# The stores of the last token group: which queue issues them, and in how many pieces

## The chip, the core and the metric

The kernel runs on one core of one Trainium2 chip. The metric is device time in microseconds for one execution of the whole program. TensorE (PE) multiplies matrices, VectorE (DVE) and ScalarE (ACT) work on elements, GpSimd (POOL) and SyncE (SP) mainly issue DMAs. A DMA is issued by an instruction on an engine's own queue (here SyncE's or ScalarE's for stores) and is then carried out by 16 DMA engines that all queues share.

## The reference

Sigmoid attention, and behind it a gated feed-forward layer, for 8 batches, 12 heads, 448 positions and 64 numbers per head:

```python
scores = scale * np.matmul(q, k.transpose(0, 1, 3, 2)) - np.log(S)
attn = 1.0 / (1.0 + np.exp(-scores))
attn_out = np.matmul(attn, v)
x = attn_out.transpose(0, 2, 1, 3).reshape(B * S, H * D)      # 3584 x 768
out = (np.maximum(x @ w_gate, 0.0) * (x @ w_val)) @ w_out     # 768 -> 1536 -> 768
```

The result is 3584 x 768 in float32, 11.0 MB.

## The kernel before, in words

Batches are taken in groups of two. For each batch the attention is computed in 16 bits (`qk_unit`, `pv_group`), and its output, transposed, feeds the gate and value products (`gv`, `gv_pair`) of the group. The gated product `hT` of a group of two batches is then multiplied by `w_out` in `down_pair`. That function takes two blocks of 128 tokens at a time (`y1` and `y2`, each a buffer of 128 x 768 float32 from a pool of four, `ysb`) and computes their column halves `lo` (0 to 384) and `hi` (384 to 768) from seven products instead of eight, with sums of the operands prepared on VectorE. ScalarE copies the first product of each half out of the accumulation bank into `y1` or `y2` (`scaled_act`, line 451), VectorE adds the others (`plus`, line 469). A later product may add onto the bank that such a copy reads, so TensorE then waits for the copy.

The order of all instructions is the order in which the Python code issues them (`manual_schedule`); each engine runs its own list from front to back. The group loop runs through `next_work`, and what remains at the end is the last group (`LAST`, batches 6 and 7): four calls of `down_pair` in a row with nothing else beside them. The first of these pairs the last block of the group before with one block of the last group; the other three take the remaining six blocks.

`store` (lines 350 to 363) writes a block to `out`. Outside the last group it is called with `(nc.sync, nc.sync)` and issues two DMAs of 64 rows each on SyncE, because the rows of the two halves lie in different places. In the last group the 128 rows of a block form one pattern. There, line 353 first removes repeated engines, and then the rows are divided among the engines that are left: `(nc.sync, nc.sync)` becomes a single DMA of 128 rows on SyncE, `(nc.sync, nc.scalar)` one DMA of 64 rows on each.

The very last `down_pair` (`last` is true) stores piece by piece, as soon as each is complete:

1. `y1` left half (line 527): SyncE, 128 rows x 384.
2. `y2` right half (line 532): SyncE 64 rows, ScalarE 64 rows, x 384.
3. `y1` right half (line 536): SyncE 64 rows, ScalarE 64 rows, x 384.
4. `y2` left half in two quarters of 192 columns, each with its own product of 12 half-width matmuls in all, its own addition on VectorE (line 545) and its own store (line 549): both on SyncE.

The stores and transposes of SyncE and ScalarE count on eight semaphores, 0 to 7, each DMA taking the next one in turn; before a semaphore is used again its earlier DMA must have landed. In the built program of this kernel, `y1`'s left half counts on number 4, `y2`'s right half on 5 and 6, `y1`'s right half on 0 (SyncE) and 7 (ScalarE), the two quarters on 1 and 2. When SyncE has issued everything it waits for these eight semaphores one after the other in the order 0 to 7, each with an instruction of its own, then drains, and the engines meet in a barrier that ends the program (line 1062 in the profile, the launch).

Of the kernel before, what the change touches and what calls it, by code (L numbers as in the profile page):

```python
# [18 lines left out]
def kernel(  # L19
# [10 lines left out]
    nc = tc.nc  # L30

    B, H, S, D = q.shape
    DM, DF = moe_w_gate.shape
# [43 lines left out]
    def bank(name, shape=(P, 512), dtype=FP32):  # L77
        pool, tag = free[0]
        free.rotate(-1)
        return pool.tile(list(shape), dtype, tag=tag, name=name)  # L80
# [4 lines left out]
    def later(order):  # L85
        keys = [free[i - 8] for i in order]
        for key in keys:
            free.remove(key)
            free.append(key)
# [260 lines left out]
    def store(g, t, ysb, m0, m1, engines):  # L350
        if g == LAST:
            dst = out[2 * g * S : 2 * (g + 1) * S, m0:m1].rearrange("(b t c) m -> c t b m", b=2, c=NCH)[t]
            engines = list(dict.fromkeys(engines))
            n = P // len(engines)
            for i, eng in enumerate(engines):
                rows = slice(i * n, (i + 1) * n)
                eng.dma_start(dst[i * n // 2 : (i + 1) * n // 2], ysb[rows, m0:m1])
            return
        for i, eng in enumerate(engines):
            j = 2 * t + i  # L360
            b, c = 2 * g + j // NCH, j % NCH
            dst = out[b * S : (b + 1) * S, m0:m1].rearrange("(t c) m -> c t m", c=NCH)[c]
            eng.dma_start(dst, ysb[64 * i : 64 * i + 64, m0:m1])
# [3 lines left out]
    HF, HM, HD = NFC // 2, DM // 2, NDC // 2  # L367
# [19 lines left out]
    def products(jobs):  # L387
        for ps, n, kn, A, W, first in jobs:
            for k_ in range(kn):
                nc.tensor.matmul(  # L390
                    ps[:, 0:n],
                    A[:, k_, :],
                    W[:, k_, :],
                    start=(first and k_ == 0),
                    stop=(k_ == kn - 1),
                    skip_group_check=True,
                )
# [21 lines left out]
    def tiles_in(g, p):  # L419
        return ((g - 1, 2 * p), (g, 2 * p)) if p == NPP else ((g, 2 * p), (g, 2 * p + 1))  # L420

    def token_blocks(g, p):
        blocks = []
        for gt, t in tiles_in(g, p):
            h = odd[gt] if gt < g else hT_tiles[g][:, :, t * P : (t + 1) * P]
            blocks += [h[:, 0:HF, :], h[:, HF:NFC, :]]
        return blocks
# [22 lines left out]
    def scaled_act(o, ps):  # L450
        nc.scalar.activation(o, ps[:, 0:HM], AF.Copy, scale=OUT_SCALE)  # L451

    def down_pair(g, p, beside, then, last, first_copy, amid=None):
        A11, A12, S3, A22 = token_blocks(g, p)
        S1, S2, S4 = sums.pop(("y", g, p))
        T1, T2, T3, T4 = late["T"]
        B11, B21, B22 = wo[:, 0:HF, 0:HM], wo[:, HF:NFC, 0:HM], wo[:, HF:NFC, HM:DM]
        y1, y2 = (ysbp.tile([P, DM], FP32, tag="ysb", name="ysb") for _ in range(2))
        lo, hi = slice(0, HM), slice(HM, DM)
        b, c = bank("u"), bank("y12")  # L460
        if not amid or (g, p) in SUMS_LATE:
            a = bank("y11")
            later((7, 6, 5))

        def product(ps, A, W, first=True):
            products([(ps, HM, HF, A, W, first)])

        def plus(o, ps):
            nc.vector.scalar_tensor_tensor(  # L469
                out=o, in0=ps[:, 0:HM], scalar=OUT_SCALE, in1=o, op0=AOP.mult, op1=AOP.add  # L470
            )

        first, second = tiles_in(g, p)

        product(b, A11, B11)
        first_copy(y1[:, lo], b)
        beside()
        if (g, p) in SUMS_LATE:
            product(a, A12, B21)
            plus(y1[:, lo], a)  # L480
            product(c, S1, T1)
            scaled_act(y2[:, hi], c)
            product(b, S2, T2, False)
            scaled_act(y1[:, hi], b)
            product(c, S4, B22, False)
            plus(y1[:, hi], c)
            store(*first, y1, 0, DM, (nc.sync, nc.sync))
            steps = ()
            if amid:
                amid()  # L490
                steps = prepare_steps()
                for step in steps[:2]:
                    step()
            product(b, S3, T3, False)
            plus(y2[:, hi], b)
            (scaled if amid else scaled_act)(y2[:, lo], b)
            d = bank("y21")
            if amid:
                later((0, 6, 7))
            else:  # L500
                then()
            product(d, A22, T4)
            plus(y2[:, lo], d)
            for step in steps[2:]:
                step()
            store(*second, y2, 0, DM, (nc.sync, nc.sync))
            return
        product(c, S1, T1)
        scaled_act(y2[:, hi], c)
        product(b, S2, T2, False)  # L510
        scaled_act(y1[:, hi], b)
        if amid:
            product(c, S4, B22, False)
            plus(y1[:, hi], c)
            amid()
            product(b, S3, T3, False)
            plus(y2[:, hi], b)
            later((0,))
            a = bank("y11")
            later((6,))  # L520
            product(a, A12, B21)
            plus(y1[:, lo], a)
        else:
            product(a, A12, B21)
            plus(y1[:, lo], a)
            if last:
                store(*first, y1, 0, HM, (nc.sync, nc.sync))
            product(b, S3, T3, False)
            plus(y2[:, hi], b)
            if last:  # L530
                scaled_act(y2[:, lo], b)
                store(*second, y2, HM, DM, (nc.sync, nc.scalar))
            product(c, S4, B22, False)
            plus(y1[:, hi], c)
        if last:
            store(*first, y1, HM, DM, (nc.sync, nc.scalar))
        else:
            store(*first, y1, 0, DM, (nc.sync, nc.sync))
        then()
        if last:  # L540
            for m0 in (0, HM // 2):
                m1 = m0 + HM // 2
                d = bank("y21")
                products([(d, HM // 2, HF, A22, T4[:, :, m0:m1], True)])
                nc.vector.scalar_tensor_tensor(
                    out=y2[:, m0:m1], in0=d[:, 0 : HM // 2], scalar=OUT_SCALE, in1=y2[:, m0:m1],
                    op0=AOP.mult, op1=AOP.add,
                )
                store(*second, y2, m0, m1, (nc.sync,))
        else:  # L550
            product(b, A22, T4, False)
            scaled_act(y2[:, lo], b)
            store(*second, y2, 0, DM, (nc.sync, nc.sync))
# [342 lines left out]
    def prepare_steps():  # L896
        if work:
            kind, g, i = work[0]
            if kind == "w":
                return unit_sum_steps(("w", g, i), i, sums_tile(2 * P))  # L900
            if kind == "y" and (g, i) != (0, 0):
                return token_sum_steps(g, i, 0, HF - 2 if FRESH.get(g) == i else HF)
        return ()
# [5 lines left out]
    def next_work(jobs=(), alone=False, amid=None, ahead=()):  # L909
        kind, g, i = work.popleft()  # L910

        due = pending[:]
        del pending[:]

        def beside():
            for job in due + list(jobs):
                job()

        for job in ahead:
            job()  # L920
        if kind == "y":
            down_pair(g, i, beside, prepare, not work, scaled_act if alone else scaled, amid)
        elif amid:
            raise ValueError(kind)
        elif kind == "w":
            by = (nc.vector.tensor_copy, nc.scalar.copy)
            gv_pair(g, i, lambda: (prepare(), beside()), (by[alone], by[alone or bool(ahead)]))
        elif kind == "s":
            gv_split(g, i, lambda: (prepare(), beside()))
        else:  # L930
            gv(g, 0, S, i, True)
            beside()
            prepare()
# [133 lines left out]
```

## Time and profile before

| | before |
|---|---|
| time, median of 3 runs | 388.93 us (388.58 to 389.41) |
| the profiled execution's own time | 388.44 us |
| its span in the profile | 386.7 us |
| TensorE busy | 380.4 us, 98% of the span |
| VectorE busy | 305.0 us, 79% |
| ScalarE busy | 227.2 us, 59% |
| GpSimd busy | 49.8 us, 13% |
| granted TensorE clock | 1.0 |
| data moved | HBM read 47.19 MB, written 11.01 MB |

A time of a run is some 1.7 us longer than the span of the same execution; what lies around the span is start and end. In the timeline a row gives the start in us from the span's start, the duration, the engine, the source line, the operation, what it writes and reads, and in brackets how long the engine stood idle before it and what released it. `SPq` and `ACTq` are the queues of SyncE and ScalarE: the duration of a `DMA_DIRECT2D` there is the time that the issuing instruction took, not the transfer. The transfer's end is seen in the list of issues as the time from issue to landing, and its data in the busy share of the DMA engines.

### The profile page before, as it was taken

Reading aid. Unit: us, or ns where it says so; the run is one execution under the profiler, and the core shown is the slowest. Engines: PE = TensorE matmul, PEld = TensorE weight load, DVE = VectorE, ACT = ScalarE, POOL = GpSimd, SP = SyncE. Lnnn points to the kernel's source line nnn. Section 1 sums busy time; section 2 is a strip of 40 time slices with the busy share of each in tenths; the row PEclk is TensorE's granted clock in tenths of the full one; section 3 lists DMA queues with packets and bytes.
Section 4 is the critical chain, followed back from the end, with each engine's and each line's share of the span. In section 5 each row is a group of like instructions: output and inputs, shape, how many; then the busy total and the mean of one; then the engine's idle time right before and its main releaser. Section 6 shows DMA issues by size and latency. Waiting matters only on the chain.

```text
span 386.7 us, 8967 instructions
## 1 busy us (share of the span) xinstructions
PE 380.4 (98%) x3570; PEld 222.9 (58%) x3570; DVE 305.0 (79%) x611; ACT 227.2 (59%) x480; POOL 49.8 (13%) x73
## 2 busy tenths in 40 slices
PE   8999999999999999999999999999999999999995
PEld 6778776885555545555555554555555555555663
DVE  3455667769868999999868789999988788999662
ACT  5967887568777645555777764555577343333321
POOL 9633307100400003000300300000000000000000
PEclk9999999999999999999999999999999999999999
DMA  9999999999979303962599892222013220000224
GB/s 179 198 199 204 203 187 163 208 208 131 186 162 178 81 2 39 165 109 47 49 231 236 157 234 44 49 49 49 0 43 83 65 60 0 2 0 2 82 102 145
DMA packets 67483, 43.81 MB, mean 113 GB/s; under 512 B 35568, under 2 KB 64112, under 8 KB 67440
## 3 DMA queue, kind: packets, MB, share of 16 engines
q0 software_dynamic: 28960, 23.24, 39.4%
q1 hardware_dynamic: 37776, 19.34, 23.6%
q10 hardware_dynamic: 704, 0.66, 0.5%
q8 instruction: 28, 0.46, 0.5%
q14 instruction: 15, 0.12, 0.1%
HBM read 47.19 MB, written 11.01 MB: 151 GB/s over the span
## 4 chain that ended last, share of the span: by engine, by line
PE 96%; ACT 2%; DMA 1%; DVE 1%; issue 0%; ACTq 0%
PE u L390 35%; PE g L390 16%; PE y L390 12%; PE qk_ps L239 10%; PE pv_ps L257 8%; PE g_ps L322 5%; PE v_ps L322 5%; PE u L719 2%; PE g L719 2%; ACT PT L187 2%; PE trt L204 1%; DMA ysb<-in_k_dram 1%; DVE qkT L211 0%; DVE q L792 0%; PE warm_ps L175 0%
## 5 line engine op out<-in xcount | busy, mean ns | idle before, releaser
L187 ACT ACTIVATE PT<-qk_ps 128x448 f16<-128x448 f32 (+3 forms) x318 | 151.0, 586 | 78.7 <-PE qk_ps L239 78.5
L390 PEld LDWEIGHTS <-S 128*128 128x128 f16 x576 | 56.3, 98 | 45.9
L629 DVE TENSOR_TENSOR gsb<-g,gsb 128x448 f32<-128x448 f32 x72 | 42.8, 624 | 7.8 <-PE g L390 7.5
L239 PE MATMUL qk_ps<-qkT 64*64 64x448 f16 (+2 forms) x756 | 47.3, 336 | 0.6 <-ACT PT L187 0.3
L390 PEld LDWEIGHTS <-hT 128*128 128x128 f16 x318 | 29.5, 98 | 24.1 <-issue 6.1
L257 PE MATMUL pv_ps<-PT,v 64*64 64x448 f16 (+2 forms) x756 | 36.4, 329 | 0.2 <-ACT PT L187 0.2
L469 DVE SCALAR_TENSOR_TENSOR ysb<-y,ysb 128x384 f32<-128x384 f32 x33 | 18.3, 556 | 20.6 <-PE y L390 14.0
L184 DVE TENSOR_SCALAR xT<-pv_ps 128x448 f16<-128x448 f32 (+2 forms) x53 | 27.8, 567 | 7.5 <-PE pv_ps L257 6.3
L390 PEld LDWEIGHTS <-wg 128*128 128x128 f16 x216 | 20.1, 98 | 21.8 <-issue 4.3
L390 PEld LDWEIGHTS <-wv 128*128 128x128 f16 x216 | 21.1, 98 | 19.7
L451 ACT ACTIVATE ysb<-u 128x384 f32<-128x384 f32 x28 | 13.7, 490 | 30.9 <-PE u L390 26.8
L390 PE MATMUL u<-wo,hT 128*128 128x384 f16 x156 | 29.8, 328 | 0.0
L239 PEld LDWEIGHTS <-qkT 64*64 64x64 f16 x756 | 17.7, 105 | 20.6 <-issue 14.0
L111 POOL DMA_DIRECT2D k<-in_k_dram x14 | 10.9, 775 | 141.4 <-DVE rel L222 135.6
L257 PEld LDWEIGHTS <-v 64*64 64x64 f16 x756 | 21.4, 107 | 11.1 <-issue 0.6
L390 PE MATMUL u<-xT,wg 128*128 128x448 f16 x108 | 23.5, 354 | 0.0
L390 PE MATMUL g<-xT,wg 128*128 128x448 f16 x108 | 23.4, 353 | 0.0
L390 PE MATMUL g<-xT,S 128*128 128x448 f16 x108 | 23.4, 353 | 0.0
L390 PE MATMUL u<-X,S 128*128 128x448 f16 x108 | 23.4, 353 | 0.0
L390 PE MATMUL g<-X,S 128*128 128x448 f16 x108 | 23.4, 353 | 0.0
L390 PE MATMUL u<-xT,wv 128*128 128x448 f16 x108 | 23.4, 353 | 0.0
L390 PE MATMUL u<-X,wv 128*128 128x448 f16 x108 | 23.4, 353 | 0.0
(98 smaller groups left out, 563.7 us busy)
## 6 DMA issues: line engine op xcount, KB each, us to landing
out_dram<-ysb SPq DMA_DIRECT2D x43, 192.0 KB, 3.6
v<-in_v_dram POOLq DMA_DIRECT2D x8, 336.0 KB, 15.6
v<-in_v_dram POOLq DMA_DIRECT2D x16, 168.0 KB, 15.6
k<-in_k_dram POOLq DMA_DIRECT2D x4, 672.0 KB, 11.8
q<-in_q_dram POOLq DMA_DIRECT2D x4, 672.0 KB, 15.2
wo<-in_moe_w_out_dram POOLq DMA_DIRECT2D x2, 1152.0 KB, 19.1
k<-in_k_dram POOLq DMA_DIRECT2D x9, 224.0 KB, 11.6
out_dram<-ysb SPq DMA_DIRECT2D x5, 384.0 KB, 2.7
```

The source lines that it names most:

```text
L111: nc.gpsimd.dma_start(t16[:, xs, cs], rows_of(src, b)[:, xs, cs])
L184: nc.vector.tensor_scalar(out=xT, in0=src, scalar1=XSCALE, scalar2=None, op0=AOP.mult)
L187: nc.scalar.activation(PT_ap, ps_ap, AF.Sigmoid, bias=sig_bias, scale=qk_scale)
L204: nc.tensor.transpose(trt[64 * h : 64 * h + 64, c * P : (c + 1) * P], t16[:, 2 * g + h, c * D : (c + 1) * D], ident[:],)
L239: nc.tensor.matmul(out_of(hh)[o : o + 64, :], qkT[rows, c, cols], qkT[rows, NCH + c0 : NCH + c1, cols], start=True, stop=True, tile_positi ...
L257: nc.tensor.matmul(ps[hh][64 * r : 64 * r + 64, 0:qn], v16[rows, 2 * g + hh, c * D : (c + 1) * D], pieces[c][rows, hh, :], start=(c == 0), ...
L322: nc.tensor.matmul(ps[:, 0:qn], (wg, wv)[i][:, dc, f * P : (f + 1) * P], xT_tiles[b][:, dc, q0 : q0 + qn], start=(dc == 0), stop=(dc == ND ...
L390: nc.tensor.matmul(ps[:, 0:n], A[:, k_, :], W[:, k_, :], start=(first and k_ == 0), stop=(k_ == kn - 1), skip_group_check=True,)
L451: nc.scalar.activation(o, ps[:, 0:HM], AF.Copy, scale=OUT_SCALE)
L469: nc.vector.scalar_tensor_tensor(out=o, in0=ps[:, 0:HM], scalar=OUT_SCALE, in1=o, op0=AOP.mult, op1=AOP.add)
L629: nc.vector.tensor_tensor(out=gs[u][i][:], in0=ps[u][:, 0:S], in1=gs[u][i][:], op=AOP.add)
L719: nc.tensor.matmul(ps[j // 2][:, j % 2 * SQ : (j % 2 + 1) * SQ], sets[j][i][:, k_, :], W[:, k_, :], start=(first and j % 2 == 0 and k_ == ...
```

## The change

Three places change. `store` no longer removes repeated engines, so `(nc.sync, nc.sync)` gives two DMAs of 64 rows each on SyncE in the last group too: that holds for its five whole blocks and for `y1`'s left half. `y1`'s right half goes as one DMA of 128 rows on SyncE. Of the two quarters of `y2`'s left half the first is stored by ScalarE, the second by SyncE as before. `y2`'s right half stays with one DMA on each.

```diff
@@ def store(g, t, ysb, m0, m1, engines):
         if g == LAST:
             dst = out[2 * g * S : 2 * (g + 1) * S, m0:m1].rearrange("(b t c) m -> c t b m", b=2, c=NCH)[t]
-            engines = list(dict.fromkeys(engines))
             n = P // len(engines)
             for i, eng in enumerate(engines):
                 rows = slice(i * n, (i + 1) * n)
@@ def down_pair(...):
         if last:
-            store(*first, y1, HM, DM, (nc.sync, nc.scalar))
+            store(*first, y1, HM, DM, (nc.sync,))
         else:
             store(*first, y1, 0, DM, (nc.sync, nc.sync))
         then()
@@
-                store(*second, y2, m0, m1, (nc.sync,))
+                store(*second, y2, m0, m1, (nc.sync if m0 else nc.scalar,))
```

In the built program SyncE then issues 15 stores in the last group instead of 10, ScalarE two as before. The instructions of TensorE, VectorE and GpSimd are the same in number and order. The semaphores move on accordingly: `y1`'s left half counts on 1 and 2, `y2`'s right half on 3 and 4, `y1`'s right half on 5, ScalarE's quarter on 6 and the last store on 7.

## The prediction

> **What bounds the kernel now.** I read the page first, then the chain of waits over the last 27 us, then every store of the last 7 us one by one.
>
> ```profile
> span 386.7 us, 8967 instructions
> PE 380.4 (98%) x3570; PEld 222.9 (58%) x3570; DVE 305.0 (79%) x611; ACT 227.2 (59%) x480; POOL 49.8 (13%) x73
> PE 96%; ACT 2%; DMA 1%; DVE 1%; issue 0%; ACTq 0%
> ...
> 380.46 1.98 PE y L390 x18
> 382.44 0.02 issue
> 382.46 0.36 DVE ysb L545
> ```
>
> TensorE is busy for 98% of the span and carries 96% of the chain. The change gives TensorE, VectorE and GpSimd no new instruction, so all but the end of these 386.7 us stays if no buffer comes free too late (last rival). The chain reaches TensorE's last product at 382.44 and VectorE's last piece at 382.82 (382.46 + 0.36). From there to 386.7 there are only stores and the end of the program: 3.9 us, the only stretch where the change can pay. Its rows, from the timeline (start, duration) and the list of DMA issues (KB, us to landing):
>
> ```profile
> 381.54 0.56 DVE L469 SCALAR_TENSOR_TENSOR ysb<-y,ysb 128x384 f32<-128x384 f32 x1 [0.43 <-PE y L390]
> 382.03 0.36 DVE L545 SCALAR_TENSOR_TENSOR ysb<-y,ysb 128x192 f32<-128x192 f32 x1
> 382.46 0.36 DVE L545 SCALAR_TENSOR_TENSOR ysb<-y,ysb 128x192 f32<-128x192 f32 x1
> ...
> 380.16 0.54 SPq L357 DMA_DIRECT2D out_dram<-ysb  x1
> 381.14 0.55 SPq L357 DMA_DIRECT2D out_dram<-ysb  x1
> 382.12 0.55 SPq L357 DMA_DIRECT2D out_dram<-ysb  x1
> 382.76 0.55 SPq L357 DMA_DIRECT2D out_dram<-ysb  x1
> 383.41 0.57 SPq L357 DMA_DIRECT2D out_dram<-ysb  x1
> 381.15 0.63 ACTq L357 DMA_DIRECT2D out_dram<-ysb  x1
> 382.13 0.57 ACTq L357 DMA_DIRECT2D out_dram<-ysb  x1
> ...
> out_dram<-ysb SPq DMA_DIRECT2D x1, 192.0 KB, 2.2
> out_dram<-ysb SPq DMA_DIRECT2D x1, 96.0 KB, 2.2
> out_dram<-ysb SPq DMA_DIRECT2D x1, 96.0 KB, 2.0
> out_dram<-ysb ACTq DMA_DIRECT2D x1, 96.0 KB, 2.4
> out_dram<-ysb ACTq DMA_DIRECT2D x1, 96.0 KB, 2.5
> ```
>
> The data of the last quarter is ready at 382.82, but SyncE issues its store at 383.41: it still has y1's half (382.12) and the quarter before (382.76) to issue, and the starts stand 0.64 and 0.65 us apart. So **SyncE's issuing is 0.59 us late**. That store lands 2.0 us on, at 385.4. Then comes the end of the program:
>
> ```profile
> L1062 SPq EVENT_SEMAPHORE  x1: 28/28/28, 384.4 to 384.4; - x1
> L1062 SPq EVENT_SEMAPHORE  x1: 28/28/28, 385.0 to 385.0; - x1
> L1062 SPq EVENT_SEMAPHORE  x6: 28/28/28, 385.5 to 385.8; - x6
> L1062 SPq DRAIN  x1: 13/13/13, 385.8 to 385.8; - x1
> ```
>
> SyncE waits for the store semaphores 0 to 7 in turn. In the built program the last store counts on number 2: the rows at 384.4, 385.0 and 385.5 are the landings on 0, 1 and 2. Numbers 3 to 7 were met earlier, yet their five waits run only now, one every 0.06 us (six from 385.5 to 385.8): **0.30 us after the last landing**.
>
> **The change part by part.** *First quarter to ScalarE.* ScalarE issued its last store at 382.13 and was free at 382.70; that store goes away, so it now meets the quarter's data (382.03 + 0.36 = 382.39) idle and issues at about 382.42. Nothing is queued behind it on ScalarE.
>
> *y1's right half in one store on SyncE.* It is issued at 382.12 as now, once for both halves: nothing added. SyncE is free at 382.67, before the last quarter is ready. In the built program one semaphore instruction now stands between VectorE's end and that store; where VectorE released a store directly, 0.02 us passed (381.54 + 0.56 to 382.12), so I take 382.88. **The last store is issued 0.53 us sooner** (bounds 0.48 to 0.56).
>
> *y1's left half in two stores.* One more issue, between 380.16 and the store at 381.14. At the spacing of 0.65 us, the widest seen here, SyncE's four stores start at 380.16, 380.81, 381.46 and 382.11: y2's right half is 0.3 us late, and y1's right half, ready at 382.10, is on time by a hair. That is the cover for this edit; each 0.1 us more per issue would put some 0.3 us on the last store.
>
> *What the transfers then cost.* The share of the 16 DMA engines in five stretches (column before the last):
>
> ```profile
> 361.80:363.60 1.80, 1.80 (x13) 1.09 (x12) 1.73 (x5) 0.77 (x2) 0.00 (x0) 1.00 0.85 217
> 365.40:366.65 1.25, 1.25 (x10) 0.73 (x9) 0.56 (x1) 0.00 (x0) 0.00 (x0) 1.00 0.80 315
> 381.35:382.10 0.75, 0.75 (x12) 0.75 (x11) 0.56 (x2) 0.28 (x1) 0.00 (x0) 1.00 0.72 262
> 382.35:383.30 0.95, 0.07 (x1) 0.00 (x0) 0.40 (x2) 0.00 (x0) 0.00 (x0) 1.00 0.76 201
> 383.35:385.15 1.80, 0.00 (x0) 0.00 (x0) 0.00 (x0) 0.00 (x0) 0.00 (x0) 1.00 0.75 215
> ...
> DMA  0018999300399879812998799796069600000000
> ```
>
> The last row cuts 381 to 386 into 40 slices of 0.125 us. The first group of digits is y1's left half as one store (0.72 x 0.75 = 0.54 us of all engines), the second y2's right half as two (0.76 x 0.95 = 0.72 us), the third y1's right half as two and both quarters (0.75 x 1.80 = 1.35 us); the single 0 in it, at 384.5, is the engines with nothing to do until the late store arrives. The third group begins at 383.3, 1.2 us after the issue at 382.12, and ends at 385.0, 0.4 us ahead of the landing. After the change it holds one store of 0.54 in place of two of 0.72, so 1.35 - 0.72 + 0.54 = 1.17 us of work. Engines full, it ends at 383.3 + 1.17 = 384.5; at the 0.75 share seen now, 383.3 + 1.17 / 0.75 = 384.9. With 0.4 us to landing: 384.9 to 385.3. By its issue alone the last store lands at 382.88 + 2.0 = 384.9. I take **385.05, a gain of 0.35** (bounds 0.1 to 0.5), nearer to full, because with both queues supplied the hole at 384.5 has no reason to stay.
>
> *The semaphore of the last store.* With five more stores ahead of it, the built program gives the last store number 7 and ScalarE's quarter number 6. All earlier waits are over before they land, so the five waits behind the landing go: **0.30 us** (0.24 if the quarter on 6 lands last).
>
> *The whole tiles in two stores.* The first two rows of the stretches above are one tile as two 64-row stores and one as a single 128-row store: 0.85 x 1.80 = 1.53 against 0.80 x 1.25 = 1.00 us of all engines. So each of these five tiles takes some 0.5 us more of the DMA engines and one more issue. The page "DMA: Bandwidth & Descriptors" of the Trainium skill, section "Rules for kernel authors", speaks against such pairs: transfers to two partition halves serialize, and one 128-partition transfer is to be used; the trace agrees with its 1.53 against 1.00. Between those stores lie tiles' worth of idle time, so I cost them at nothing:
>
> ```profile
> 368.47 0.55 SPq L357 DMA_DIRECT2D out_dram<-ysb  x1
> 369.31 0.54 SPq L357 DMA_DIRECT2D out_dram<-ysb  x1
> 376.13 0.54 SPq L357 DMA_DIRECT2D out_dram<-ysb  x1
> 376.59 0.49 ACT L451 ACTIVATE ysb<-u 128x384 f32<-128x384 f32 x1 [0.48 <-PE u L390]
> 377.37 0.33 PE L390 MATMUL u<-T,S 128*128 128x384 f16 x1
> out_dram<-ysb SPq DMA_DIRECT2D x1, 384.0 KB, 3.1
> DMA to landing us min/median/max: 2.0/2.9/10.0
> ```
>
> The last whole tile is issued at 376.13; even 1.5 us later and with the 3.1 us that the slowest of these stores took, it has landed by 380.7, before the data of y1's left half flows (381.3).
>
> **Sum:** 0.35 + 0.30 = 0.65 us off the profiled execution's 388.44 (387.79). The runs' median is 388.93, 0.49 above that execution; the same 0.65 off it is **388.28 us**, 0.17% faster. The bound of what a measurement of this kernel can tell from no change, 0.2%, is 0.78 us: the forecast lies just inside it.
>
> **Rivals.** *The queues drain quickly.* The quarters leave on two queues at 382.42 and 382.88 and neither waits for the other: the last lands 2.0 us after an issue at 382.85, at 384.85. Gain 0.55 + 0.30 = 0.85 us, 388.08. For it: the one store that went alone had the shortest time to landing, 2.0, and the work allows 384.9. Against: the quarters now overlap with y1's half, and stores beside others took 2.2 to 2.5.
>
> *The transfers are the bound.* The engines were 75% busy in the last stretch; if the last store, issued sooner, only queues longer, the data still ends near 385.0 and just the semaphore order pays: 0.30 us and little more, 388.6. The sum's 1.17 against 1.35 us of work speaks against it, ScalarE's slow start (2.4 and 2.5 to landing) for it. The Trainium skill, same page, section "Issuing engines are not separate DMA queues", has this rule: DMAs from several engines run on the same 16 and save only issue time. By it and the row above the issue time is worth saving only where the engines stand idle, which here is the 0 at 384.5.
>
> *A buffer comes free too late: slower.* ScalarE's copy at 376.59 writes the output buffer whose stores start at 368.47. With two stores each, the second starts near 369.1, and both must have landed. The product at 377.37 adds onto the bank that this copy reads, so TensorE stalls once the copy ends after 377.37, that is, once a store takes over 7.7 us (376.88 - 369.1). The longest store of the whole run took 10.0: landing at 379.1, copy done at 379.6, TensorE 2.2 us late, less 0.65: 1.6 us slower, 390.5. Against it: that 10.0 stands beside a median of 2.9, and the stores of the last group took at most 3.1, with no loads left to disturb them.
>
> That the change doesn't do what it says is ruled out by the built program: SyncE has ten 32x2x768, three 32x2x384, one 64x2x384 and one 64x2x192 stores, ScalarE one 32x2x384 and one 64x2x192.
>
> **How the numbers follow.** Forecast (gain 0.4 to 0.75) 0.45; quick queues (0.75 to 0.95) 0.34; transfers bound (0.2 to 0.4) 0.15; late buffer 0.06. The medians of three runs scatter by some 0.2 us (388.58 to 389.41 for single runs), so a third of the forecast and four fifths of the quick case come out beyond 0.78: 0.15 + 0.27, and 0.02 from the third, 0.44 faster. Slower is the last case, 0.06; the rest, 0.50, is within 0.2%. The range takes the first three cases with that scatter: 387.7 to 388.8.
>
> **What would show it.** Right: SyncE's last store issued at 382.9, ScalarE's quarter at 382.4, no empty slice in the last group of DMA digits, the last landing near 385.05, and one wait ahead of the drain in place of six. The issue step is wrong if y1's right half starts later than 382.15. The transfer step is wrong if the last landing stays at 385.3 or later, and the semaphore step if waits still follow it. The whole is wrong if TensorE's last product ends at another time than 382.4, or the time between drain and end differs.

## The result, and the profile after

| | before | after |
|---|---|---|
| median | 388.82 us (12 runs, 388.2 to 389.84) | 388.03 us (12 runs, 387.47 to 388.3) |
| ratio | | 0.9976, 95% interval 0.9967 to 0.9985 |
| profiled execution, and its span | 388.44 us, 386.7 us | 388.30 us, 386.5 us |
| end of VectorE's last piece | 382.82 us | 383.43 us |
| from there to the end of the span (the tail) | 3.84 us | 3.10 us |

The medians differ by 0.79 us, 0.2%; the forecast was 0.65 us. The two profiled executions differ by only 0.14 us, and the table shows why: the tail is 0.74 us shorter, but VectorE's last piece ends 0.61 us later. The page and the end of the chain of the changed kernel:

```profile
span 386.5 us, 8978 instructions
PE 381.1 (99%) x3570; PEld 223.2 (58%) x3570; DVE 304.9 (79%) x611; ACT 227.3 (59%) x480; POOL 49.8 (13%) x73
...
381.07 1.98 PE y L389 x18
383.04 0.02 issue
383.07 0.36 DVE ysb L544
```

Those 0.61 us arise long before the first store that was changed. Compared instruction by instruction, TensorE in this execution is 0.53 us behind that of before already after 10 us, 0.23 behind from 34 to 202 us, 0.61 behind at 213 us, and then 0.61 behind to the last product, to 0.01 us. The waits of TensorE between 195 and 215 us name the last step; the kernel of before has no row there:

```profile
PE qk_ps L239 <- DMA qkT<-rel: 0.3, 1, 0.3
```

So executions differ in when input loads and one transposing DMA arrive, and the change is read in the tail.

That the change has no part in the step at 212 us is not shown. In the nine traces kept here, taken against the kernel before, it stands in all six whose whole blocks go in two stores (0.15 to 0.74 us), and neither in the kernel before nor in the two others with whole blocks in one store (under 0.01 us). The instructions up to there are the same, and the first store that differs is issued some 150 us later; what would link the two is open. The times do not settle it. Set beside the change of its tail, a kernel's median is between 0.07 us too fast and 0.39 us too slow with the blocks in two, and 0.18 too fast and 0.32 too slow in the two kernels without.

The stores of the last pair in the changed kernel, from the timeline and the DMA issues:

```profile
382.15 0.56 DVE L468 SCALAR_TENSOR_TENSOR ysb<-y,ysb 128x384 f32<-128x384 f32 x1 [0.43 <-PE y L389]
382.64 0.36 DVE L544 SCALAR_TENSOR_TENSOR ysb<-y,ysb 128x192 f32<-128x192 f32 x1
383.07 0.36 DVE L544 SCALAR_TENSOR_TENSOR ysb<-y,ysb 128x192 f32<-128x192 f32 x1
...
380.77 1.17 SPq L356 DMA_DIRECT2D out_dram<-ysb  x2
382.04 0.55 SPq L356 DMA_DIRECT2D out_dram<-ysb  x1
382.73 0.60 SPq L356 DMA_DIRECT2D out_dram<-ysb  x1
383.49 0.55 SPq L356 DMA_DIRECT2D out_dram<-ysb  x1
381.76 0.66 ACTq L356 DMA_DIRECT2D out_dram<-ysb  x1
383.03 0.56 ACTq L356 DMA_DIRECT2D out_dram<-ysb  x1
...
out_dram<-ysb SPq DMA_DIRECT2D x1, 192.0 KB, 2.3
out_dram<-ysb ACTq DMA_DIRECT2D x1, 96.0 KB, 2.3
out_dram<-ysb SPq DMA_DIRECT2D x1, 96.0 KB, 2.1
```

The last store is issued 0.06 us after its data is ready (383.07 + 0.36 = 383.43, to 383.49), where it was 0.59 us. ScalarE issues the first quarter at 383.03, as soon as VectorE ends it at 383.00. The semaphore waits of SyncE at the end, cut into short windows, and the busy digits of the DMA engines from 381.6 to 386.6 in 40 slices, with the share of one stretch:

```profile
L1061 SPq EVENT_SEMAPHORE  x6: 27/28/28, 384.1 to 384.4; - x6
L1061 SPq EVENT_SEMAPHORE  x1: 28/28/28, 385.1 to 385.1; - x1
L1061 SPq EVENT_SEMAPHORE  x1: 28/28/28, 385.4 to 385.4; - x1
L1061 SPq EVENT_SEMAPHORE  x1: 28/28/28, 385.6 to 385.6; - x1
L1061 SPq DRAIN  x1: 7/7/7, 385.7 to 385.7; - x1
...
DMA  0027995069979988992599989999800000000000
383.95:385.30 1.35, 0.00 (x0) 0.00 (x0) 0.00 (x0) 0.00 (x0) 0.00 (x0) 1.00 0.89 291
```

Six waits are over by 384.4, before anything late has landed. Then come three landings, y1's right half, ScalarE's quarter and the last store, and behind the last of them directly the drain. Before, five waits stood in between. The hole in the digits ahead of the last store is gone: from the first data of y1's right half to the last data the engines are 89% busy, where they were 75%.

In the records of the two traces, counted from the end of VectorE's last piece, the last landing (read here and below at the start of the wait that it ends, 0.02 us behind the landing itself) moved from 2.63 to 2.22 us, the drain from 3.00 to 2.28, the end from 3.84 to 3.10.

### The profile page after: what moved, and what is told of

Same layout as the page of the kernel before. It is cut to its first block, busy times and chain, and to the rows that moved or that the text cites. A ratio compares the mean times of both kernels' runs of the same rounds, so it can differ in the third digit from the quotient of the medians.

```text
span 386.5 us, 8978 instructions
## 1 busy us (share of the span) xinstructions
PE 381.1 (99%) x3570; PEld 223.2 (58%) x3570; DVE 304.9 (79%) x611; ACT 227.3 (59%) x480; POOL 49.8 (13%) x73
## 4 chain that ended last, share of the span: by engine, by line
PE 96%; ACT 2%; DMA 1%; DVE 0%; issue 0%
PE u L389 34%; PE g L389 16%; PE y L389 12%; PE qk_ps L239 10%; PE pv_ps L257 8%; PE g_ps L322 5%; PE v_ps L322 5%; PE u L718 2%; PE g L718 2%; ACT PT L187 2%; DMA qkT<-rel 1%; PE warm_ps L175 1%; PE trt L204 1%; DVE ysb L544 0%; DVE zeros L130 0%
```

## The experiments

Each experiment is read by its tail, because the tail repeated in the one case that was tried: the changed kernel profiled a second time (last experiment) had 3.10 us again, while that execution took 0.2 us longer. One profiled execution stands behind each of the other tails.

| kernel | last issue after VectorE's end | last landing | waits behind it | tail | ratio to before, 95% interval |
|---|---|---|---|---|---|
| before | 0.59 | 2.63 | 5 | 3.84 | |
| changed | 0.06 | 2.22 | 0 | 3.10 | 0.9976 (0.9967 to 0.9985) |
| engine edits alone | 0.06 | 2.17 | 6 | 3.42 | 0.9984 (0.9975 to 0.9992) |
| blocks in two alone | 0.58 | 2.60 | 0 | 3.49 | 0.9998 (0.9988 to 1.0009) |
| changed, blocks whole | 0.06 | 2.27 | 5 | 3.46 | 1.0001 (0.9988 to 1.0014) |
| one more issue | 1.22 | 3.23 | 0 | 4.14 | 1.0013 (1.0002 to 1.0023) |
| full height | 0.06 | 2.16 | 0 | 3.07 | 0.9980 (0.9971 to 0.9989) |
| y1's right in halves | 0.06 | 2.54 | 1 | 3.48 | 0.9987 (0.9978 to 0.9996) |
| changed again | 0.06 | 2.21 | 0 | 3.10 | 0.9980 (0.9971 to 0.9989) |

(us from the end of VectorE's last piece; in the last row but one the last landing is that of ScalarE's quarter.)

**The engine edits alone.** To the kernel before:

```diff
-            store(*first, y1, HM, DM, (nc.sync, nc.scalar))
+            store(*first, y1, HM, DM, (nc.sync,))
...
-                store(*second, y2, m0, m1, (nc.sync,))
+                store(*second, y2, m0, m1, (nc.sync if m0 else nc.scalar,))
```

> Only the two engine edits: y1's right half in one store on SyncE, the first quarter on ScalarE; whole blocks and y1's left half stay one store each. Read by the tail, from the end of VectorE's last piece to the end of the span: 3.84 us before, 3.09 us in the changed kernel. The last store counts on semaphore 1, so six waits follow it. Theory (SyncE issues the last store 0.53 us sooner, and each semaphore wait behind the last landing costs 0.06 us): tail 0.42 shorter by the landing and 0.06 longer by one more wait, 3.45 to 3.5 us, 0.35 us faster than before. Rival 1 (the DMA engines are the bound, an earlier issue only queues longer): 3.9 us, nothing gained. Rival 2 (the gain comes from the blocks going out in two pieces): 3.84 us.

Its last piece, last store, and waits in the half microsecond up to the drain:

```profile
382.16 0.36 DVE L545 SCALAR_TENSOR_TENSOR ysb<-y,ysb 128x192 f32<-128x192 f32 x1
382.58 0.54 SPq L357 DMA_DIRECT2D out_dram<-ysb  x1
L1062 SPq EVENT_SEMAPHORE  x7: 28/28/28, 384.7 to 385.1; - x7
L1062 SPq DRAIN  x1: 7/7/7, 385.1 to 385.1; - x1
```

The issue is as early as in the changed kernel, and the landing comes 0.47 us sooner than before. Of the seven waits the first is the landing and six follow, over some 0.37 us. The tail of 3.42 is 0.43 below before, where 0.35 was expected, and just under the expected 3.45 to 3.5: the landing gained 0.05 us more than the 0.42 taken over from the changed kernel. Rival 1 (3.9) and rival 2 (3.84) both fall.

**The blocks in two alone.** To the kernel before:

```diff
-            engines = list(dict.fromkeys(engines))
+            if m1 - m0 < DM:
+                engines = list(dict.fromkeys(engines))
```

> Only the five whole blocks of the last group go in two stores each; the last block pair is stored as before. This moves the last store from semaphore 2 to semaphore 7 and issues it no sooner. Theory: tail 3.84 - 5 x 0.06 = 3.54 us, 0.30 us faster than before, no wait between the last landing and the drain. Rival 1 (transfers are the bound and only the semaphore order pays): the same 3.54. Rival 2 (the pieces carry the gain): 3.1 us, 0.74 us faster. If the extra 0.5 us of DMA work for each block were not hidden, the TensorE products of the last three pairs would start later than 6.83 us apart.

```profile
384.46 0.36 DVE L546 SCALAR_TENSOR_TENSOR ysb<-y,ysb 128x192 f32<-128x192 f32 x1
385.40 0.56 SPq L358 DMA_DIRECT2D out_dram<-ysb  x1
L1063 SPq EVENT_SEMAPHORE  x1: 28/28/28, 387.4 to 387.4; - x1
L1063 SPq DRAIN  x1: 7/7/7, 387.5 to 387.5; - x1
```

Nothing is issued sooner (385.40 is 0.58 behind 384.82), one wait stands ahead of the drain in place of six, and the tail is 3.49, close to the 3.54 expected from the order of the semaphores and far from rival 2's 3.1. That five more stores, whose data needs no splitting, shorten the end by 0.35 us is the part of the change that its text shows least. The time shows none of it: this kernel's runs go from 387.79 to 390.09, and its interval of 0.9988 to 1.0009 holds both no change and the 0.9991 that the tail makes. The profiled execution is its longest run, and shows where such scatter comes from; the row is from TensorE's waits in the first 40 us:

```profile
PE v_ps L322 <- DMA wv<-in_moe_w_val_dram: 1.5, 1, 1.5
```

TensorE waited 1.5 us for a weight. After 213 us its distance to the kernel before does not change by more than 0.01 us, so the extra DMA work of the blocks in two is hidden.

**The changed kernel with whole blocks.** To the changed kernel:

```diff
             dst = ...
+            if m1 - m0 == DM:
+                engines = engines[:1]
```

> The changed kernel with its five whole blocks in one store each; y1's left half in two and the two engine edits stay. The last store counts on semaphore 2 as before, so five waits follow it. Theory: tail 3.84 - 0.42 = 3.4 us, 0.42 us faster than before and 0.33 us slower than the changed kernel. Rival 1: 3.84 us. Rival 2 (whole blocks in two pieces carry the gain): 3.84 us.

```profile
382.39 0.36 DVE L546 SCALAR_TENSOR_TENSOR ysb<-y,ysb 128x192 f32<-128x192 f32 x1
382.81 0.55 SPq L358 DMA_DIRECT2D out_dram<-ysb  x1
L1063 SPq EVENT_SEMAPHORE  x6: 28/28/28, 385.0 to 385.3; - x6
```

Six waits again, the landing and five behind it, and a tail of 3.46, where 3.4 was expected: 0.36 us longer than in the changed kernel, for 0.33. Both rivals' 3.84 falls. Against the engine edits alone only y1's left half differs, in two stores here. The last landing is 0.10 us later for it (2.27 against 2.17). So this edit is not free. Its two half stores take 0.86 us of all DMA engines where one takes 0.53. That agrees with the rule of the Trainium skill, "DMA: Bandwidth & Descriptors", section "Rules for kernel authors", against two transfers to partition halves. Whether this work or the added issue costs the 0.10 us was not separated; the records point to the issue. The data of y1's left half is through 0.21 us before VectorE's end. But SyncE's part of y2's right half leaves 0.31 us later than with the engine edits alone, its data flows until 0.57 us after VectorE's end in place of 0.18, and y1's right half, next on the same queue, begins at 0.58 in place of 0.50. The median of this kernel did not move, and its interval, 0.14% to the slow side and 0.12% to the fast, just holds the tail's 0.10%.

**One more issue on SyncE.** To the kernel with the blocks in two:

```diff
-            if m1 - m0 < DM:
+            if m1 - m0 < DM and m0 == 0:
                 engines = list(dict.fromkeys(engines))
...
-            store(*first, y1, HM, DM, (nc.sync, nc.scalar))
+            store(*first, y1, HM, DM, (nc.sync, nc.sync))
```

> The run with the five blocks in two stores, and y1's right half as two stores that are both on SyncE; both quarters on SyncE. The last store stays on semaphore 7. So SyncE has four issues in place of three between 382.1 and the end. Theory (SyncE's issuing is the bound): the last store is issued 0.58 to 0.65 us later than before, 1.2 us after VectorE's last piece, tail 3.54 + 0.6 = 4.1 to 4.2 us, 0.3 us slower than before. Rival 1 (the DMA engines are the bound): issued later but landing at the same time, tail 3.54 us.

```profile
383.59 0.36 DVE L546 SCALAR_TENSOR_TENSOR ysb<-y,ysb 128x192 f32<-128x192 f32 x1
385.17 0.56 SPq L358 DMA_DIRECT2D out_dram<-ysb  x1
out_dram<-ysb SPq DMA_DIRECT2D x1, 96.0 KB, 2.0
L1063 SPq EVENT_SEMAPHORE  x1: 28/28/28, 387.2 to 387.2; - x1
```

The same bytes, the same semaphore, one issue more on SyncE: the last store goes out 0.64 us later and lands 0.63 us later, and the tail is 4.14, within the 4.1 to 4.2 expected. The time follows (1.0013, interval above 1). Here SyncE's issuing, not the DMA engines, sets the last landing.

**Full height.** To the changed kernel:

```diff
+            if t == 2 * NPP:
+                engines = (nc.sync,) * 4
             n = P // len(engines)
...
-                store(*first, y1, 0, HM, (nc.sync, nc.sync))
+                store(*first, y1, 0, HM, (nc.sync,))
...
-                store(*second, y2, HM, DM, (nc.sync, nc.scalar))
+                store(*second, y2, HM, DM, (nc.scalar,))
```

> The changed kernel with full-height stores for the last pair: y1's left half in one store on SyncE, y2's right half in one store on ScalarE; the block of the first pair goes in four stores, so that the last store keeps semaphore 7. Issue time and number of waits behind the last landing as in the changed kernel; the DMA engines' work ahead of the last store falls by some 0.3 us for each pair of half stores made one (0.86 to 0.53 and 0.73 to 0.53). Theory: the last store still meets a queue in the changed kernel (2.15 us from issue to landing, against 2.04 for the lone one of before), so the tail falls from 3.10 to 3.0 to 3.05 us. Rival (those 2.15 us are the store's own time, with no queue in them): 3.10 us. Time: the same as the changed kernel within what a measurement can tell.

The tail is 3.07, between the two expectations: the last store now takes 2.10 us to land instead of 2.15, so half of the queue that I supposed was there. The ratio to before is 0.9980 for this kernel and for the changed one beside it. The tail is 0.03 us shorter than in the changed kernel, and in the time nothing of that can be seen (medians of 388.30 and 388.07).

**y1's right half in halves again.** To the changed kernel:

```diff
-                store(*first, y1, 0, HM, (nc.sync, nc.sync))
+                store(*first, y1, 0, HM, (nc.sync,))
...
-            store(*first, y1, HM, DM, (nc.sync,))
+            store(*first, y1, HM, DM, (nc.sync, nc.scalar))
```

> The changed kernel with y1's right half again as one half store on SyncE and one on ScalarE, and y1's left half as one store, so that the last store stays on semaphore 7; the first quarter stays on ScalarE. Takes the one-store edit alone away. SyncE issues the last store as early as in the changed kernel, ScalarE issues the first quarter 0.3 us later. Theory (issue time and semaphore order carry the gain; the half stores add 0.2 us of DMA work): tail 3.15 to 3.3 us, at most 0.2 us slower than the changed kernel. Rival (putting y1's right half into one store is what shortens the last landing): the data ends where it did before, tail 3.5 us.

```profile
382.99 0.36 DVE L544 SCALAR_TENSOR_TENSOR ysb<-y,ysb 128x192 f32<-128x192 f32 x1
383.41 0.55 SPq L356 DMA_DIRECT2D out_dram<-ysb  x1
383.32 0.79 ACTq L356 DMA_DIRECT2D out_dram<-ysb  x1
L1061 SPq EVENT_SEMAPHORE  x2: 28/28/28, 385.9 to 385.9; - x2
```

My expectation of 3.15 to 3.3 was wrong: the tail is 3.48, the rival's figure. The last store on SyncE is as early as ever. What lands last is ScalarE's quarter: ScalarE was busy with y1's half and issued the quarter at 383.32, 0.36 us later than in the changed kernel, and it took 2.57 us to land, in place of 2.3. So putting y1's right half into one store matters, above all because it takes the store away that kept ScalarE from the quarter. SyncE's last store, issued at the same distance, lands only 0.06 us later than in the changed kernel, and 0.11 later than with the engine edits alone, whose last pair differs in y1's right half only. So much at most is the saved DMA work. The reverse, y1's right half in one store with both quarters on SyncE, was not run.

**The changed kernel again.**

> The changed kernel once more, beside the other two: tail 3.10 us, time 0.7 to 0.8 us below before. All of any further difference in its time must stand before the last group, since TensorE's last pairs start 6.83 us apart in every kernel here.

Tail 3.10, median 388.07 against 388.88 for before in the same job: 0.81 us.

## Why the prediction was right, point by point

- *Only the end can change.* In all these traces TensorE's distance to the kernel before is constant from 213 us on; the buffers came free in time, and the slower rival did not occur. But the sign set for this, TensorE's last product ending at 382.4, failed: it ended at 383.05, for the 0.61 us from before 213 us. All other times of the prediction are met only when they are counted from VectorE's last piece. The profiled execution, forecast at 387.79, took 388.30.
- *The last store is issued 0.53 us sooner.* 0.53 (0.59 to 0.06).
- *y1's right half on time, y2's right half 0.3 us late.* 382.73 for data ready at 382.71, and 382.04 for data ready at about 381.72. The starts stand 0.58 us apart on y1's left half and then 0.70, together 1.27 for the 1.30 allowed.
- *Transfers: 1.17 us of work, landing gain 0.35 us.* The work was 0.89 x 1.35 = 1.20 us and the gain 0.42. This is the term that was mis-sized, by 0.07 us. About half of that is the landing of before, which I took as 383.41 + 2.0 = 385.4 from a rounded row; the records have it at 385.43. The rest is that the landing forecast 2.23 us after VectorE's end (385.05) came at 2.20 (2.22 as the table counts). Against it, y1's left half in two was costed as an issue that the later stores absorb; it put the last landing 0.1 us back between the two runs with whole blocks in one store.
- *The whole blocks in two, costed at nothing.* Nothing came of them at the end, but not for the reason given. The prediction let them land within 3.1 us, by 380.7, which is 2.1 us before VectorE's end. The two stores of the last block, issued at 377.18 and 377.77, took over 4 us and landed as late as 1.3 us before it:

```profile
out_dram<-ysb SPq DMA_DIRECT2D x2, 192.0 KB, 4.4
```

  In the run with the blocks in two alone it was 0.95 us before it, with the block's last data flowing until 0.02 us after y1's left half began. In the repeat it was 1.69 us before, and the tail was the same. So there is less room than the prediction thought. Why these two take so long is open: in the changed kernel's records an instruction fetch of 16 KB holds one DMA engine for 1.5 us among them, but the kernel before has such a fetch too, of 1.0 us, when its last whole block is nearly through.
- *Semaphore order: 0.30 us.* 0.30: the drain follows the last landing by 0.065 us where it was 0.37.
- The stretch from drain to end, costed as unchanged, was 0.02 us shorter.

The sum of the tail is 0.42 us at the landing (of 0.53 at the issue), 0.30 and 0.02: 0.74 us against 0.65. The measured 0.79 and 0.81 lie just on the other side of 0.2% from the forecast, with an interval of 0.15% to 0.33% that holds the tail's 0.19%. That medians and tail agree to 0.07 us here is in part luck: in the other kernels they differ by 0.03 to 0.39 us. The forecast time of 388.28 us came out at 388.03; 0.11 of the difference is the median of before, 388.82 with twelve runs in place of 388.93 with three. Of the rivals, "the queues drain quickly" asked for 2.0 us from issue to landing and got 2.15; "the transfers are the bound" is refuted by the engine edits alone, where the store issued 0.53 us sooner landed 0.47 us sooner, and by the run with one more issue.

## What to carry to other kernels

Read the end of a program by itself: which instruction issues the last store, how long after its data is ready, and what the issuing engine still does after it has landed. Two queues are worth having there when one engine's issues stand end to end, and the last transfer should count on the semaphore that is waited for last. Where the effect is a few tenths of a microsecond and the start of the program scatters by more, measure from a common late event in the trace, and not by the time alone.

## What the runs showed of the hardware that was not expected

Two stores issued at almost the same moment on SyncE and ScalarE do not start together. In all nine cases in which a store on ScalarE was issued within 0.1 us of one on SyncE, its first data came 1.62 to 1.64 us after issue, while SyncE's came after 1.19 to 1.25. In the nine others, with about 0.3 us or more between them, ScalarE's came after 1.31 to 1.49 us. In the run with y1's right half in halves this adds 0.15 us to the 0.36 by which ScalarE's quarter is issued later.

Of the two half-height stores of one column half that leave on the two queues, the one that starts first moves slowly, whichever half it is: of y2's right half, SyncE's rows 0 to 63 took 0.46 us of all DMA engines before and ScalarE's rows 64 to 127 took 0.28, while in the changed kernel ScalarE's started first and took 0.46, and SyncE's 0.27. Two in a row on SyncE were both slow: y1's left half took 0.86 us as two stores and 0.53 as one, for the same bytes. Why is open.
